# Attention and a routed MLP on one core: scores on 64 rows, whole key tiles per engine, no shifts on GpSimd

## The chip, the cores and the metric

The kernel runs on one core of a Trainium2 chip. The metric is the device time of one execution in microseconds (us). Engines are called TensorE (PE in profile rows, its weight loads PEld), VectorE (DVE), ScalarE (ACT), GpSimd (POOL) and SyncE (SP, which issues the DMAs).

## The reference, cut to what matters

```python
x = A_x                                   # [1, 2048, 448], bf16
xn = layernorm(x)
q = (xn @ wq) -> 16 heads of 28           # k = xn @ wk, v = xn @ wv: ONE key/value head of 28
scores = einsum("bhqd,bkd->bhqk", q, k) * 28 ** -0.5
o = softmax(scores) @ v -> [2048, 448]
h = x + o @ wo
n = layernorm(h); r = n @ w_r             # B: the 8 rows with the largest r go through a gated MLP
out = h + n + scatter(MLP(n[top8]) * sigmoid(r[top8]))
```

All 16 heads share one K and one V. Nearly all of the work is in the scores, their exponentials and the products with V: 16 heads x 2048 queries x 2048 keys.

## The kernel before, in words

**Tiling.** A block b (16 of them, in order) is one group of four heads and 512 queries. Within a block j counts 16 key tiles of 128 keys and i the four heads. So a head tile (b, j, i) is a score tile of 128 keys x 512 queries, which fills one PSUM bank, and there are 1024 of them. Head i of a group sits on partitions 32i to 32i+31 of `Q`; 28 of these 32 rows are the head, one is a constant row that carries an offset. `K` holds K four times, once for each 32 rows. `qk()` is the score matmul of a head tile: 32 rows of K (stationary, 128 columns) against 32 rows of Q (moving, 512 columns).

**Two ways to the exponential.** Tiles of the list `act_tiles` (744) go in pairs through `act_unit`: two `qk()` into two neighbouring banks (0 and 1, or 2 and 3), and one ScalarE exponential over both (line 582) into one of NPB = 8 buffers `P`. Tiles of `dve_tiles` (280) go through `dve_tile`, one at a time, into bank 4 or 5 in turn; VectorE clamps the scores into 16-bit integers that are read as bf16 (line 596, tile `Y`). Four of these make a batch (`dve_batch`), from which three shifted copies are made, each one instruction over 2048 columns (`shift`, line 601): `v == 1`, and `v == 2` in every second batch, on GpSimd, the others on VectorE. The four heads and three key tiles of a batch are spread by a fixed pattern, so every key tile of most blocks has tiles of both kinds.

**Products with V.** Each is a matmul with 128 rows and 32 stationary columns (V with a column of ones, 28 columns of V, zeros); four of them, one for each head i, lie side by side on the columns of the array and are one operation. `act_pv` does this for four tiles of `P`, `dve_pv` for the four tiles of a batch and one of its four copies. They accumulate in bank 6 or 7 (`acc_bank`). That makes 744 + 4 x 280 = 1864 matmuls in 466 groups of four.

**Around the blocks.** `chunk(c)` prepares a quarter of the rows (layer norm, transposes, K, V); its part 0 runs ahead of the first block, the others during it. `q_project` makes Q two blocks ahead. `post_block` moves the sums out of PSUM, inverts the row sums through small DMAs to DRAM and back, and multiplies on GpSimd (line 498). `out_proj` runs for four row tiles after every fourth block, mostly on VectorE. After the last block come the last `out_proj`, the choice of the eight rows, their MLP and the output.

**Order of the work.** `_Graph.op` records every operation with an engine, an assumed duration, its reads and writes, and a priority (its due time, in units of one key tile). `plan()` lays them out as a list schedule and fixes each engine's order; `emit` writes that order out with semaphore waits. So each engine runs a fixed sequence, and an instruction that waits holds up all behind it on its engine. A second, exact program is built behind a flag and runs only when row sums leave a range.

Of the kernel before, what the change touches and what calls it, by code (L numbers as in the profile page):

```python
# [18 lines left out]
class _Op:  # L19
    __slots__ = ("eng", "fns", "dur", "lat", "deps", "prio", "idx", "dma", "start", "end", "sig", "name", "nsucc",  # L20
                 "pred_left", "succs", "ready")


class _Graph:
# [16 lines left out]
    def op(self, eng, fns, dur, reads=(), writes=(), prio=None, dma=False, acc=False, name=""):  # L41
# [34 lines left out]
        return o  # L76

    def plan(self):
# [15 lines left out]
        seq = []  # L94
        while left:
# [18 lines left out]
            c.end = s + c.dur  # L114
            free[e] = c.end
# [109 lines left out]
def _main(nc, G, sb, ps, psb, flag, scr, A_x, A_wq, A_wk, A_wv, A_wo, B_w_r, B_w_gate, B_w_up, B_w_down, out,  # L225
          exact=False):
    S, D, H, C = A_x.shape[1], A_x.shape[2], 16, 8
    DH = D // H
# [4 lines left out]
    NPB = 8  # L233
# [30 lines left out]
    kb = sb("kb", [128, 1], F32)  # L264
    wo_pad = sb("wo_pad", [128, 4, D], BF16)
    Q = sb("Q", [128, 4, 512], BF16)
    K = sb("K", [128, S], BF16)
# [88 lines left out]
    for i in range(4, NT, 4):  # L356
# [64 lines left out]
    def chunk(c):  # L421
# [22 lines left out]
        for t0 in (4 * c, 4 * c + 2):  # L444
# [9 lines left out]
            else:  # L454
# [116 lines left out]
    def qk(bank, tile):  # L571
        b, j, i = tile
        return mm(ps[:, bank, :], K[32 * i:32 * i + 32, j * 128:(j + 1) * 128], Q[32 * i:32 * i + 32, b % 4, :],
                  True, True)

    def act_unit(n, unit):
        b0, sl = 2 * (n % 2), n % NPB
        t = unit[0][0] * 16 + unit[0][1] + unit[0][2] / 8
        G.op(PE, [qk(b0 + k, u) for k, u in enumerate(unit)], 260,
             reads=sorted({("Q", b % 4) for b, j, i in unit}) + sorted({("K", j // 4) for b, j, i in unit}),  # L580
             writes=[pk(b0), pk(b0 + 1)], prio=t - 3)
# [3 lines left out]
    def act_pv(lst):  # L585
        b = lst[0][1][0]
        G.op(PE, [mm(ps[32 * i:32 * i + 32, acc_bank(b), :], Vs[:, 0, j, :], P[:, (n // 2) % NPB, n % 2, :], f, l)
                  for n, (_, j, i), f, l in lst], 260,
             reads=sorted({("P", n // 2 % NPB) for n, *_ in lst}) + sorted({("V", t[1] // 4, 0) for _, t, *_ in lst}),
             writes=[pk(acc_bank(b))])  # L590

    def dve_tile(m, b, j, i):
        n, k, bank = m // 4 % NY, m % 4, 4 + m % 2
        t = b * 16 + j
        G.op(PE, qk(bank, (b, j, i)), 90, reads=[("Q", b % 4), ("K", j // 4)], writes=[pk(bank)], prio=t - 2.9)
        G.op(DV, lambda e: e.tensor_scalar(Y[:, n, 0, k, :].bitcast(I16), ps[:, bank, :], 0.0, 32639.0 - 3 * STEP,  # L596
                                           ALU.max, ALU.min), 610, reads=[pk(bank)], writes=[("Y", n, 0, k)],
             prio=t - 2)
# [12 lines left out]
    def dve_pv(v, lst):
        m, (b, _, _) = lst[0][:2]
        n = m // 4 % NY
        G.op(PE, [mm(ps[32 * i:32 * i + 32, acc_bank(b), :], Vs[:, v + 1, j, :], Y[:, n, v, m % 4, :], f, l)
                  for m, (_, j, i), f, l in lst], 260,
             reads=[("Y", n, v, k) for k in range(4)] + sorted({("V", t[1] // 4, v + 1) for _, t, *_ in lst}),
             writes=[pk(acc_bank(b))])

    for n in range(0, len(act_tiles), 2):
        at(16 * act_tiles[n][0] + act_tiles[n][1] + 0.1, act_unit, n // 2, act_tiles[n:n + 2])  # L620
    quads = []
    for n, tile in enumerate(act_tiles):
        for q in quads[-3:]:
            if len(q) < 4 and q[0][1][0] == tile[0] and all(t[2] != tile[2] for _, t in q):
                q.append((n, tile))
                break
        else:
            quads.append([(n, tile)])
    for q in quads:
        b, j, i = q[-1][1]  # L630
        pv_list.append((16 * b + j + 1.2, 0, 0, q))
    for m in range(0, len(dve_tiles), 4):
        for k in range(4):
            b, j, i = dve_tiles[m + k]
            at(16 * b + j + 0.15, dve_tile, m + k, b, j, i)
        at(16 * b + j + 0.2, dve_batch, m)
        for v in (0, 3, 2, 1):
            pv_list.append((16 * b + j + (3.2 if v == 0 else 3.7 if v == 3 else 4.2 if v == 2 else 4.7), 1, v,
                            [(m + k, dve_tiles[m + k]) for k in range(4)]))
    pv_list.sort(key=lambda t: t[0])  # L640
    first, last = {}, {}
    for n, (tp, kind, v, lst) in enumerate(pv_list):
        for q, e_ in enumerate(lst):
            b, j, i = e_[-1]
            first.setdefault((b, i), (n, q))
            last[b, i] = (n, q)
    for n, (tp, kind, v, lst) in enumerate(pv_list):
        full = [e_ + (first[e_[-1][0], e_[-1][2]] == (n, q), last[e_[-1][0], e_[-1][2]] == (n, q))
                for q, e_ in enumerate(lst)]
        if kind:  # L650
            at(tp, dve_pv, v, full)
        else:
            at(tp, act_pv, full)
# [11 lines left out]
    if exact:  # L665
# [214 lines left out]
```

## Time and profile before

| | |
|---|---|
| median of 3 runs (lowest to highest) | 589.13 us (580.43 to 589.92) |
| the profiled execution | 585.16 us, span 583.3 us |
| TensorE, share of the span busy | 84% |
| VectorE | 72% |
| ScalarE | 65% |
| GpSimd | 43% |
| mean granted clock of TensorE | 0.694 of full speed |

The span runs from the first to the last instruction; the profiled execution takes 1.86 us more than its span. The granted clock of TensorE is 1.00 for 2.4 GHz and 0.50 for 1.2 GHz; other values are means over a stretch with both. A matmul's busy time includes the time to run through the array, so busy TensorE is not TensorE at its peak.

### The profile page before, as it was taken

Reading aid. Unit: us, or ns where it says so; the run is one execution under the profiler, and the core shown is the slowest. Engines: PE = TensorE matmul, PEld = TensorE weight load, DVE = VectorE, ACT = ScalarE, POOL = GpSimd, SP = SyncE. Lnnn points to the kernel's source line nnn. Section 1 sums busy time; section 2 is a strip of 40 time slices with the busy share of each in tenths; the row PEclk is TensorE's granted clock in tenths of the full one; section 3 lists DMA queues with packets and bytes.
Section 4 is the critical chain, followed back from the end, with each engine's and each line's share of the span. In section 5 each row is a group of like instructions: output and inputs, shape, how many; then the busy total and the mean of one; then the engine's idle time right before and its main releaser. Section 6 shows DMA issues by size and latency. Waiting matters only on the chain.

```text
span 583.3 us, 8246 instructions
## 1 busy us (share of the span) xinstructions
PE 487.5 (84%) x3384; PEld 120.7 (21%) x3384; DVE 419.5 (72%) x765; ACT 377.3 (65%) x403; POOL 251.0 (43%) x167
## 2 busy tenths in 40 slices
PE   1889988888797999999896898989998889943286
PEld 1332111221121111112221221211222211111151
DVE  6896256897779875758988888778888876625613
ACT  1586897987667865659776896756569765533102
POOL 6124043767414564426644575563524664320000
PEclk9885577987668665558876995765559865566555
DMA  8900000000000000000000000000000000000003
GB/s 235 269 22 0 21 0 17 5 21 2 19 1 12 9 3 20 0 13 9 21 1 20 1 21 1 20 1 16 6 3 18 2 20 1 20 5 17 1 1 130
DMA packets 15940, 14.64 MB, mean 25 GB/s; under 512 B 5960, under 2 KB 12888, under 8 KB 15896
## 3 DMA queue, kind: packets, MB, share of 16 engines
q1 hardware_dynamic: 15896, 14.05, 8.3%
q8 instruction: 28, 0.46, 0.3%
q14 instruction: 16, 0.13, 0.1%
HBM read 11.94 MB, written 2.10 MB: 24 GB/s over the span
## 4 chain that ended last, share of the span: by engine, by line
PE 60%; DVE 28%; ACT 7%; issue 2%; DMA 1%; POOL 1%; SPq 0%; POOLq 0%; DVEq 0%
PE ps L333 59%; DVE Y L596 9%; DVE Y L601 9%; ACT P L582 6%; DVE junk L547 1%; DMA x_sb<-in_A_x_dram 1%; DVE bn L516 1%; DVE Ot L486 1%; DVE hbuf L514 1%; DVE bn L426 1%; DVE xn L441 1%; DVE Lmn L491 1%; DVE st L530 1%; DVE Q L418 0%; DVE idx L729 0%
## 5 line engine op out<-in xcount | busy, mean ns | idle before, releaser
L582 ACT ACTIVATE P<-ps 128x1024 bf16<-128x1024 f32 x372 | 362.3, 1028 | 140.1 <-PE ps L333 137.6
L601 POOL TENSOR_SCALAR Y<-Y 128x2048 int16<-128x2048 int16 x102 | 206.0, 2032 | 154.7 <-DVE Y L596 154.1
L333 PE MATMUL ps<-Q,K 32*128 32x512 bf16 x1024 | 233.5, 492 | 39.0 <-DVE Y L596 23.5
L596 DVE TENSOR_SCALAR Y<-ps 128x512 int16<-128x512 f32 x280 | 183.3, 681 | 90.0 <-PE ps L333 88.6
L333 PE MATMUL ps<-Y,Vs 128*32 128x512 bf16 x1120 | 133.4, 515 | 3.3 <-DVE Y L601 3.3
L601 DVE TENSOR_SCALAR Y<-Y 128x2048 int16<-128x2048 int16 x108 | 118.8, 1120 | 0.6
L333 PE MATMUL ps<-P,Vs 128*32 128x512 bf16 x744 | 96.2, 512 | 3.0 <-DVE st L518 3.0
L333 PEld LDWEIGHTS ps<-Q,K 32*128 32x128 bf16 x1024 | 46.0, 96 | 230.1 <-ACT P L582 97.7
L498 POOL TENSOR_TENSOR On<-Ot,Rb 128x512 bf16<-128x512 f32 x16 | 22.3, 1392 | 57.8 <-DMA Rb<-l_scr 57.8
L333 PEld LDWEIGHTS ps<-Y,Vs 128*32 128x32 bf16 x1120 | 29.9, 106 | 70.1 <-issue 54.3
L333 PEld LDWEIGHTS ps<-P,Vs 128*32 128x32 bf16 x744 | 20.1, 100 | 66.0 <-issue 61.4
L333 PE MATMUL ps<-wo_pad,On 128*128 128x448 bf16 x64 | 22.6, 501 | 7.2 <-POOL On L498 7.2
L333 PE MATMUL ps<-xnT,wq_pad 112*128 112x512 bf16 x64 | 26.0, 511 | 0.8 <-DVE Ot L486 0.7
L526 POOL TENSOR_TENSOR st<-st,nhalf 128x1 f32<-128x1 f32 x12 | 6.5, 543 | 39.3 <-DVE st L518 39.3
L514 DVE TENSOR_TENSOR hbuf<-ps,x_sb 128x448 f32<-128x448 f32 x16 | 9.8, 611 | 14.3 <-PE ps L333 14.3
L336 PE MATMUL ps<-ident,xn 128*112 128x128 bf16 x64 | 6.7, 271 | 11.8 <-POOL vone L383 10.7
L418 DVE TENSOR_SCALAR Q<-ps,qone 128x512 bf16<-128x512 f32 x16 | 11.7, 731 | 6.0 <-PE ps L333 6.0
L486 DVE COPY Ot<-ps 128x512 f32<-128x512 f32 x15 | 10.3, 684 | 6.3 <-PE ps L333 6.2
L547 DVE SCALAR_TENSOR_TENSOR junk<-hbuf,st,w_rb 128x448 bf16<-128x448 f32 x16 | 14.3, 892 | 0.0
L491 DVE TENSOR_TENSOR Lmn<-Lmn,Lc 128x16 f32<-128x16 f32 x16 | 8.2, 510 | 7.7 <-DMA Lc<-l_scr 7.7
L792 ACT ACTIVATE xnT<-ps 128x448 bf16<-128x448 f32 x8 | 4.3, 543 | 13.1 <-PE ps L333 13.1
L426 DVE BATCH_NORM_STATS2 bn<-x_sb 128x6 f32<-128x448 bf16 x16 | 9.3, 603 | 4.6 <-DMA x_sb<-in_A_x_dram 4.6
(120 smaller groups left out, 185.9 us busy)
## 6 DMA issues: line engine op xcount, KB each, us to landing
Rb<-l_scr SPq DMA_DIRECT2D x16, 256.0 KB
out_dram<-xnT SPq DMA_DIRECT2D x4, 448.0 KB, 3.4
wg_sb<-in_B_w_gate_dram SPq DMA_DIRECT2D x1, 1568.0 KB, 11.9
wu_sb<-in_B_w_up_dram SPq DMA_DIRECT2D x1, 1568.0 KB, 17.6
wd_sb<-in_B_w_down_dram SPq DMA_DIRECT2D x1, 1568.0 KB, 21.5
x_sb<-in_A_x_dram SPq DMA_DIRECT2D x3, 448.0 KB, 6.5
x_sb<-in_A_x_dram SPq DMA_DIRECT2D x2, 224.0 KB, 2.8
wq_sb<-in_A_wq_dram SPq DMA_DIRECT2D x1, 392.0 KB, 5.3
```

What stands on the lines that cost most here:

```text
L333: return lambda e: e.matmul(o, lhsT=l, rhs=r, start=start, stop=stop)
L336: return lambda e: e.transpose(o, i, ident[0:p, 0:p])
L418: G.op(DV, lambda e: e.tensor_scalar(Q[:, b % 4, :], ps[:, bank, :], qone[:, 0:1], None, ALU.add), dvt(512), reads=[pk(bank), "qone"], wri ...
L426: G.op(DV, [lambda e, t=t: e.bn_stats(bn6[:, t, :], x_sb[:, t, :])], dvt(D), reads=[("x", t)], writes=[("bn6", t)])
L486: (lambda e: e.tensor_copy(Ot[:, rb, :], ps[:, acc_bank(b), :])), dvt(512), reads=[pk(acc_bank(b))],
L491: G.op(DV, lambda e: e.tensor_tensor(Lmn[:, :], Lmn[:, :], Lc[:, rb, :], ALU.min), 85, reads=["Lmn", ("Lc", rb)], writes=["Lmn"])
L498: G.op(PO, lambda e: e.tensor_tensor(On[:, qb % 2, g, :], Ot[:, rb, :], Rb[:, rb, :], ALU.mult), 1270, reads=[("Ot", rb), ("Rb", rb)], wri ...
L514: G.op(DV, lambda e: e.tensor_tensor(hbuf[:, hr, :], ps[:, bank, 0:D], x_sb[:, t, :], ALU.add), dvt(D), reads=[pk(bank), ("x", t)], writes ...
L547: G.op(DV, lambda e: e.scalar_tensor_tensor(junk[:, :], hbuf[:, hr, :], st[:, t, 4:5], w_rb[:, :], ALU.mult, ALU.mult, accum_out=st[:, t, ...
L582: G.op(AC, lambda e: e.activation(P[:, sl, :, :], ps[:, b0:b0 + 2, :], ACT.Exp, bias=EBIAS, scale=OCT), 905, reads=[pk(b0), pk(b0 + 1)], w ...
L596: G.op(DV, lambda e: e.tensor_scalar(Y[:, n, 0, k, :].bitcast(I16), ps[:, bank, :], 0.0, 32639.0 - 3 * STEP, ALU.max, ALU.min), 610, reads ...
L601: G.op(eng, lambda e: e.tensor_scalar(Y[:, n, v, :, :].bitcast(I16), Y[:, n, 0, :, :].bitcast(I16), 1.0, v * STEP, ALU.mult, ALU.add), 210 ...
```

## The change

Four things change.

1. **Scores on 64 rows.** `K` becomes two tensors of 128 partitions, `K[:, 0, :]` and `K[:, 1, :]`. In copy p, of each 64 partitions only the 32 that belong to a head of parity p hold K, the other 32 hold zeros. A score matmul takes 64 rows of K and 64 rows of Q (two heads); the zeros take out the head that isn't meant. Two matmuls, on partitions 0 to 63 and 64 to 127, make the scores of heads p and p + 2 and are one operation.
2. **Whole key tiles per engine.** Of each block some key tiles belong to VectorE with all four heads, the others to ScalarE. `groups` gives four such tiles to most blocks, three to blocks 4, 8 and 12, none to block 0: 57 key tiles, 228 head tiles, on VectorE; 199 key tiles, 796 head tiles, on ScalarE. A ScalarE key tile is two `act_unit`s (p = 0, 1), a VectorE key tile two `dve_unit`s, each a pair of scores into banks 4 and 5 and two clamps.
3. **Products with V** are made for the four heads of one key tile at once.
4. **No shifts on GpSimd.** All three shifts of a VectorE key tile run on VectorE, as an addition of a constant.

Beside that NPB falls from 8 to 6; the copies of K take eight operations (one on ScalarE) where there were four; a few one-column operations prepare their scales; and the planner adds 100 ns where TensorE goes from one form (scores, products, other) to another.

```diff
-    NPB = 8
+    NPB = 6
...
+            if e == PE:
+                if form != c.form:
+                    c.end += 100.0
+                form = c.form
...
+    G.op(DV, lambda e: e.tensor_single_scalar(pid2[:, :], pidx[:, :], 63, ALU.bitwise_and), 70, reads=["pidx"],
+         writes=["pid2"])
...
+    for p in range(2):
+        G.op(DV, lambda e, p=p: e.tensor_scalar(ksc[:, p:p + 1], pid2[:, :], 32, KSCALE,
+                                                ALU.is_ge if p else ALU.is_lt, ALU.mult), 70, reads=["pid2"],
+             writes=[("ksc", p)])
+        G.op(DV, lambda e, p=p: e.tensor_scalar(kb[:, p:p + 1], pid2[:, :], DH + 32 * p, ZERO, ALU.is_equal, ALU.mult),
+             70, reads=["pid2"], writes=[("kb", p)])
...
-        G.op(DV, lambda e, bank=bank, c=c: e.tensor_scalar(K[:, c * 512:(c + 1) * 512], ps[:, bank, :], KSCALE, kb[:, 0:1],
-                                                           ALU.mult, ALU.add), dvt(512),
-             reads=[pk(bank), "kb0"], writes=[("K", c)])
+        for p in range(2):
+            if c == 0 and p == 0:
+                G.op(AC, lambda e, bank=bank, p=p: e.activation(K[:, p, 0:512], ps[:, bank, :], ACT.Identity,
+                                                                bias=kb[:, p:p + 1], scale=ksc[:, p:p + 1]), 640,
+                     reads=[pk(bank), ("kb", p), ("ksc", p)], writes=[("K", c, p)])
+            else:
+                G.op(DV, lambda e, bank=bank, c=c, p=p: e.tensor_scalar(
+                    K[:, p, c * 512:(c + 1) * 512], ps[:, bank, :], ksc[:, p:p + 1], kb[:, p:p + 1],
+                    ALU.mult, ALU.add), 670, reads=[pk(bank), ("kb", p), ("ksc", p)], writes=[("K", c, p)])
...
-    triples = [(0, 1, 2, 3, 4)] * NB
-    triples[0] = ()
-    triples[1] = (0, 2, 4)
+    groups = [4] * NB
+    groups[0] = 0
     for b in range(4, NB, 4):
-        triples[b] = (0, 1, 2, 4)
+        groups[b] = 3
+    where = {0: (), 1: (9,), 2: (5, 11), 3: (3, 7, 11), 4: (1, 5, 9, 13)}
...
+    def qk(bank, b, j, p):
+        return [mm(ps[:, bank + k, :], K[64 * k:64 * k + 64, p, j * 128:(j + 1) * 128],
+                   Q[64 * k:64 * k + 64, b % 4, :], True, True) for k in range(2)]
...
+    def act_pv(n, b, j, f, l):
+        G.op(PE, [mm(ps[32 * i:32 * i + 32, acc_bank(b), :], Vs[:, 0, j, :], P[:, (2 * n + i % 2) % NPB, i // 2, :], f, l)
+                  for i in range(4)], 216,
+             reads=[("P", 2 * n % NPB), ("P", (2 * n + 1) % NPB), ("V", j // 4, 0)], writes=[pk(acc_bank(b))], form=2)
+
+    def dve_unit(m, b, j, p, t):
+        n = m % NY
+        G.op(PE, qk(4, b, j, p), 216, reads=[("Q", b % 4), ("K", j // 4, p)], writes=[pk(4), pk(5)], prio=t - 2.9,
+             form=1)
+        for k in range(2):
+            G.op(DV, lambda e, k=k: e.tensor_scalar(Y[:, n, 0, p + 2 * k, :].bitcast(I16), ps[:, 4 + k, :], 0.0,
+                                                    32639.0 - 3 * STEP, ALU.max, ALU.min), 610, reads=[pk(4 + k)],
+                 writes=[("Y", n, 0, p + 2 * k)], prio=t - 2)
+
+    def shift(m, v):
+        n = m % NY
+        G.op(DV, lambda e: e.tensor_scalar(Y[:, n, v, :, :].bitcast(I16), Y[:, n, 0, :, :].bitcast(I16),
+                                           v * STEP, None, ALU.add), 610,
              reads=[("Y", n, 0, k) for k in range(4)], writes=[("Y", n, v, k) for k in range(4)])
...
+    for n, (b, j, t) in enumerate(act_tiles):
+        for p in range(2):
+            at(t + 0.6 * p, act_unit, 2 * n + p, b, j, p, t + 0.6 * p)
+        pv_list.append((t + 2.0, act_pv, n, b, j))
+    for m, (b, j, t) in enumerate(dve_tiles):
+        for p in range(2):
+            at(t + 1.5 * p, dve_unit, m, b, j, p, t + 1.5 * p)
         for v in (1, 2, 3):
+            at(t + 1.6 + 0.5 * v, shift, m, v)
+        for v in range(4):
+            pv_list.append((t + 2.2 + 0.5 * v, dve_pv, m, v, b, j))
```

## Rows read from the trace of the kernel before

**Rows 1.** The page: span, busy time of each engine, chain that ended last.
```profile
span 583.3 us, 8246 instructions
...
PE 487.5 (84%) x3384; PEld 120.7 (21%) x3384; DVE 419.5 (72%) x765; ACT 377.3 (65%) x403; POOL 251.0 (43%) x167
...
PE 60%; DVE 28%; ACT 7%; issue 2%; DMA 1%; POOL 1%; SPq 0%; POOLq 0%; DVEq 0%
```
**Rows 2.** Windows: stretch, length, busy time (instructions), granted clock, DMA share, GB/s.
```profile
321.50:352.20 30.70, 27.20 (x251) 7.09 (x248) 27.69 (x42) 26.88 (x28) 20.07 (x10) 1.00 0.03 10
208.90:266.90 58.00, 56.93 (x314) 9.81 (x313) 36.48 (x57) 33.62 (x35) 26.15 (x15) 0.50 0.03 11
99.70:120.10 20.40, 16.34 (x168) 4.37 (x166) 17.48 (x24) 19.18 (x20) 14.08 (x7) 1.00 0.04 14
300.00:320.00 20.00, 14.85 (x103) 3.73 (x99) 18.48 (x51) 14.13 (x16) 7.87 (x8) 0.78 0.05 16
```
**Rows 3.** Groups by line, 208.9 to 266.9 us: count, busy us, mean ns, idle before.
```profile
L333 PE MATMUL ps<-Q,K 32*128 32x512 bf16 x102 | 30.1, 604 | 1.1 <-DVE Y L596 0.6 <-ACT P L582 0.3
```
**Rows 4.** The same group, 321.5 to 352.2 us.
```profile
L333 PE MATMUL ps<-Q,K 32*128 32x512 bf16 x83 | 16.6, 390 | 2.2 <-DVE Y L596 1.2 <-ACT P L582 0.8
```
**Rows 5.** Timeline: the first and the last exponential on ScalarE.
```profile
19.02 1.02 ACT L582 ACTIVATE P<-ps 128x1024 bf16<-128x1024 f32 x1 [6.23 <-PE ps L333]
...
514.16 1.02 ACT L582 ACTIVATE P<-ps 128x1024 bf16<-128x1024 f32 x1 [0.42 <-PE ps L333]
```
**Rows 6.** Windows of TensorE, only instructions that read Q: the scores.
```profile
79.00:82.60 3.60, 1.26 (x6) 0.50 0.00 0
82.60:86.00 3.40, 2.14 (x12) 1.00 0.00 0
478.50:482.00 3.50, 1.82 (x11) 0.99 0.00 0
235.00:239.60 4.60, 3.27 (x12) 0.50 0.00 0
```
**Rows 7.** Windows of TensorE, only instructions that read Vs: the products with V.
```profile
79.00:82.60 3.60, 2.54 (x24) 0.50 0.00 0
82.60:86.00 3.40, 1.06 (x12) 1.00 0.00 0
```
**Rows 8.** TensorE near the end of the span: a timeline row, and a window.
```profile
562.63 5.09 PE L333 MATMUL ps<-wd_sb,guT 128*8 128x448 bf16 x14 [1.02 <-DVE guT L775]
...
567.30:568.40 1.10, 0.41 (x2) 1.00 0.00 0
```
**Rows 9.** Timeline of TensorE at 2.4 GHz: start, length, what.
```profile
341.10 0.39 PE L333 MATMUL ps<-P,Vs 128*32 128x512 bf16 x4
...
341.31 0.39 PE L333 MATMUL ps<-Y,Vs 128*32 128x512 bf16 x4
...
341.63 0.39 PE L333 MATMUL ps<-Q,K 32*128 32x512 bf16 x2
```
**Rows 10.** Timeline of TensorE at 1.2 GHz.
```profile
68.36 0.61 PE L333 MATMUL ps<-Q,K 32*128 32x512 bf16 x2 [0.31 <-ACT P L582]
68.90 0.62 PE L333 MATMUL ps<-P,Vs 128*32 128x512 bf16 x4
```
**Rows 11.** The page: exponentials, shifts and clamps over the whole span.
```profile
L582 ACT ACTIVATE P<-ps 128x1024 bf16<-128x1024 f32 x372 | 362.3, 1028 | 140.1 <-PE ps L333 137.6
L601 POOL TENSOR_SCALAR Y<-Y 128x2048 int16<-128x2048 int16 x102 | 206.0, 2032 | 154.7 <-DVE Y L596 154.1
...
L596 DVE TENSOR_SCALAR Y<-ps 128x512 int16<-128x512 f32 x280 | 183.3, 681 | 90.0 <-PE ps L333 88.6
...
L601 DVE TENSOR_SCALAR Y<-Y 128x2048 int16<-128x2048 int16 x108 | 118.8, 1120 | 0.6
```
**Rows 12.** Timeline of VectorE: the last three shifts, with GpSimd at rest.
```profile
511.44 1.90 DVE L601 TENSOR_SCALAR Y<-Y 128x2048 int16<-128x2048 int16 x3
```
**Rows 13.** Timeline of VectorE: the first copy of K.
```profile
15.64 0.75 DVE L461 TENSOR_SCALAR K<-ps,kb 128x512 bf16<-128x512 f32 x1 [0.79 <-PE ps L333]
```

More of the change, by code (lines that the diff above doesn't have):

```diff
@@ L20 @@
     __slots__ = ("eng", "fns", "dur", "lat", "deps", "prio", "idx", "dma", "start", "end", "sig", "name", "nsucc",
-                 "pred_left", "succs", "ready")
+                 "pred_left", "succs", "ready", "form")
 class _Graph:
@@ L39, in __init__, with op @@
         self.orders = None
-    def op(self, eng, fns, dur, reads=(), writes=(), prio=None, dma=False, acc=False, name=""):
+    def op(self, eng, fns, dur, reads=(), writes=(), prio=None, dma=False, acc=False, name="", form=0):
         o = _Op()
@@ L49, in op @@
         o.sig = False
+        o.form = form
         def need(p, sem):
@@ L94, in plan @@
         seq = []
+        form = 0
         while left:
@@ L263, in _main @@
     qone = sb("qone", [128, 1], F32)
-    kb = sb("kb", [128, 1], F32)
+    kb = sb("kb", [128, 2], F32)
+    ksc = sb("ksc", [128, 2], F32)
+    pid2 = sb("pid2", [128, 1], I32)
     wo_pad = sb("wo_pad", [128, 4, D], BF16)
     Q = sb("Q", [128, 4, 512], BF16)
-    K = sb("K", [128, S], BF16)
+    K = sb("K", [128, 2, S], BF16)
     Vs = sb("Vs", [128, NV, NT, 32], BF16)
@@ L552, in out_proj @@
              reads=[("st6", t), "sw", ("st2", t)], writes=[("r", t)])
-    triples = [(0, 1, 2, 3, 4)] * NB
-    triples[0] = ()
-    triples[1] = (0, 2, 4)
+    groups = [4] * NB
+    groups[0] = 0
     for b in range(4, NB, 4):
-        triples[b] = (0, 1, 2, 4)
+        groups[b] = 3
+    where = {0: (), 1: (9,), 2: (5, 11), 3: (3, 7, 11), 4: (1, 5, 9, 13)}
     dve_tiles, act_tiles = [], []
     for b in range(NB):
+        d = where[groups[b]]
         for j in range(NT):
-            for i in range(4):
-                on_dve = j < 15 and j // 3 in triples[b] and (j % 3, i) in ((0, 2), (1, 1), (2, 0), (2, 3))
-                (dve_tiles if on_dve else act_tiles).append((b, j, i))
+            if j in d:
+                dve_tiles.append((b, j, 16.0 * b + j - 0.5))
+            else:
+                act_tiles.append((b, j, 16.0 * (b + (j - sum(k < j for k in d)) / (NT - len(d)))))
     events = [(4.0 * c - 9.0, lambda c=c: chunk(c)) for c in range(4)]
@@ L569, in at, with act_unit @@
         events.append((t, lambda: fn(*a)))
[L571 to L576, printed above, removed]
+    def qk(bank, b, j, p):
+        return [mm(ps[:, bank + k, :], K[64 * k:64 * k + 64, p, j * 128:(j + 1) * 128],
+                   Q[64 * k:64 * k + 64, b % 4, :], True, True) for k in range(2)]
+    def act_unit(n, b, j, p, t):
@@ L577, in act_unit @@
         b0, sl = 2 * (n % 2), n % NPB
[L578 to L581, printed above, removed]
+        G.op(PE, qk(b0, b, j, p), 216, reads=[("Q", b % 4), ("K", j // 4, p)], writes=[pk(b0), pk(b0 + 1)],
+             prio=t - 3, form=1)
         G.op(AC, lambda e: e.activation(P[:, sl, :, :], ps[:, b0:b0 + 2, :], ACT.Exp, bias=EBIAS, scale=OCT),
@@ L583, in act_unit @@
              905, reads=[pk(b0), pk(b0 + 1)], writes=[("P", sl)], prio=t)
[L585 to L598, printed above, removed]
@@ L600, in shift @@
-    def shift(n, v, eng):
-        G.op(eng, lambda e: e.tensor_scalar(Y[:, n, v, :, :].bitcast(I16), Y[:, n, 0, :, :].bitcast(I16), 1.0,
-                                            v * STEP, ALU.mult, ALU.add), 2100 if eng == PO else 610,
-             reads=[("Y", n, 0, k) for k in range(4)], writes=[("Y", n, v, k) for k in range(4)])
-    def dve_batch(m):
-        n, q = m // 4 % NY, m // 4
-        last = q >= len(dve_tiles) // 4 - 2
-        for v in (1, 2, 3):
-            shift(n, v, PO if (v == 1 or (v == 2 and q % 2)) and not last else DV)
@@ L611, in dve_pv @@
[L611 to L639, printed above, removed]
@@ L640, in _main @@
-    pv_list.sort(key=lambda t: t[0])
[L641 to L653, printed above, removed]
+    def act_pv(n, b, j, f, l):
+        G.op(PE, [mm(ps[32 * i:32 * i + 32, acc_bank(b), :], Vs[:, 0, j, :], P[:, (2 * n + i % 2) % NPB, i // 2, :], f, l)
+                  for i in range(4)], 216,
+             reads=[("P", 2 * n % NPB), ("P", (2 * n + 1) % NPB), ("V", j // 4, 0)], writes=[pk(acc_bank(b))], form=2)
@@ new lines, in shift, with dve_pv @@
+    def shift(m, v):
+        n = m % NY
+        G.op(DV, lambda e: e.tensor_scalar(Y[:, n, v, :, :].bitcast(I16), Y[:, n, 0, :, :].bitcast(I16),
+                                           v * STEP, None, ALU.add), 610,
+             reads=[("Y", n, 0, k) for k in range(4)], writes=[("Y", n, v, k) for k in range(4)])
+    def dve_pv(m, v, b, j, f, l):
+        n = m % NY
+        G.op(PE, [mm(ps[32 * i:32 * i + 32, acc_bank(b), :], Vs[:, v + 1, j, :], Y[:, n, v, i, :], f, l)
+                  for i in range(4)], 216,
+             reads=[("Y", n, v, k) for k in range(4)] + [("V", j // 4, v + 1)], writes=[pk(acc_bank(b))], form=2)
@@ L654, in _main @@
+    pv_list.sort(key=lambda t: t[0])
     done = {}
-    for tp, kind, v, lst in pv_list:
-        done[lst[0][1][0]] = tp
+    for n, e_ in enumerate(pv_list):
+        b = e_[-2]
+        at(e_[0], e_[1], *e_[2:], b not in done, n == max(k for k, q in enumerate(pv_list) if q[-2] == b))
+        done[b] = e_[0]
     for b in range(NB):
@@ L676, in _main @@
                     nx += 1
-                    G.op(PE, [mm(ps[:, c, :], Q[rows, b % 4, k * 128:(k + 1) * 128], K[rows, c * 512:(c + 1) * 512],
+                    G.op(PE, [mm(ps[:, c, :], Q[rows, b % 4, k * 128:(k + 1) * 128], K[rows, i % 2, c * 512:(c + 1) * 512],
                                  True, True) for c in range(4)], 1000,
-                         reads=[("Q", b % 4)] + [("K", c) for c in range(4)], writes=[pk(c) for c in range(4)])
+                         reads=[("Q", b % 4)] + [("K", c, i % 2) for c in range(4)], writes=[pk(c) for c in range(4)])
                     G.op(DV, lambda e, r2=r2: e.tensor_reduce(nmax[:, r2:r2 + 1], ps[:, 0:4, :], AX.XY, ALU.max,
```

2 lines of the change are left out of this document (removed).

## The prediction

> **What bounds the kernel now.** I read the page first: busy shares and the chain that ended last. TensorE is busy 487.5 of 583.3 us and carries 60% of the chain, VectorE 28%, ScalarE 7% [rows 1]. An average over stretches with different limits says little, so the windows came next, cut where the granted clock of TensorE changes [rows 2]. From 208.9 to 266.9 us the clock is 1.2 GHz and TensorE is busy 56.9 of 58.0 us, ScalarE 33.6: TensorE alone is the bound. From 321.5 to 352.2 us it is 2.4 GHz, and VectorE (27.7 of 30.7 us), TensorE (27.2) and ScalarE (26.9) are all nearly full, so none is.
>
> What the clock is worth follows from the score matmuls in these stretches, one for each head tile: 102 in 58.0 us is 0.569 us a tile at 1.2 GHz [rows 2, 3], 83 in 30.7 us is 0.370 us at 2.4 GHz [rows 2, 4]. The loop over the blocks runs from the first exponential at 19.0 to the end of the last at 515.2 us [rows 5], 496 us for 1024 tiles. All at 1.2 GHz it would take 582 us, all at 2.4 GHz 379; 496 lies at a share of 0.58 of the tiles at 1.2 GHz. So the loop is set by its clock more than by any one engine, and the change has to be judged at each level, and then by what it does to the share.
>
> **The clock.** What did TensorE do before it rose or fell? From 79.0 to 82.6 us the clock was low and TensorE spent 2.5 us in products with V (128 rows) and 1.3 us in scores (32 rows); at 82.6 it rose [rows 6, 7]. In the next 3.4 us it did 2.1 us of scores and 1.1 us of products [rows 6, 7], and the clock fell. The stretch 478.5 to 482.0 us, nearly all scores, ended in a fall as well [rows 6]. From 235.0 to 239.6 us there were 3.3 us of scores, two thirds of the time, and the clock stayed low [rows 6]; so it did through the whole of 208.9 to 266.9 us, at 98% busy [rows 2]. Near the end of the span 14 matmuls of 448 columns took 5.09 us, 0.36 us each, which is the low level; they use 128 rows but only 8 stationary columns, and behind them the clock stood at 2.4 GHz [rows 8]. So in this trace rises come behind stretches with many rows at work, falls behind stretches of 32-row scores. After the change a pair of scores works on all 128 rows (64 and 64), half of them against zeros. I read this as: the scores will look like the products do now. The trace can't show whether zeros in the stationary operand take that away; the 8-column row is the nearest, and speaks for rows rather than filled cells.
>
> The Trainium skill (TensorE: Matmul & The Clock Gate, Why this matters for your kernels) says that for the full clock TensorE is to be kept busy without a break. The 58 us at 98% busy and 1.2 GHz don't agree with that alone. By that rule the change, which takes work from TensorE, would do nothing for the clock; that is the first rival below.
>
> **The change part by part.**
>
> *Scores and products on TensorE.* A turn from one form to another costs time: at 2.4 GHz one group of four products follows another after 0.21 us, but scores follow products after 0.32 us [rows 9], so a turn is 0.11 us. At 1.2 GHz products follow scores after 0.54 us [rows 10], 0.43 us without the turn. For 64-row scores no row exists. Bounds: side by side as the 32-row pair now (one slot a pair, [rows 9]) or one after the other (two slots). I take one slot, since the two halves share no rows and the row is of the same kind. Slots after: 512 pairs of scores, 199 + 57 x 4 = 427 groups of products (466 before), 64 Q projections and 48 output projections inside the loop: 1051. Turns: two for each group of products at most, 854; some groups stand together, so I take 700, 77 us (0 to 94). At 2.4 GHz that is 1051 x 0.21 + 77 = 298 us, beside ScalarE and off the path. At 1.2 GHz it is 1051 x 0.43 + 77 = 529, with 2% of waits [rows 2] 540 us, against 582 before.
>
> The Trainium skill (TensorE: Matmul & The Clock Gate, Measured speedup vs the span model) gives 3.07 times for four 32-row tiles side by side, which 64 rows rule out: scores at that rate would be an estimated 70 us where 512 x 0.21 gives 108. In the trace pairs are what the kernel issues, so that is not lost now; at 2.4 GHz it would be off the path anyway.
>
> *ScalarE.* 796 head tiles are 398 exponentials where there were 372. At 2.4 GHz 28 of them took 26.88 us, 0.96 each [rows 2]; 398 make 382 us. This is the largest load of any engine, so at 2.4 GHz ScalarE sets the loop. How full can it be? 0.88 in one stretch at 2.4 GHz and 0.94 in another [rows 2]. I take 0.93, near the better, because VectorE, which was just as full there, is relieved; 0.88 and 0.97 are the ends. 382 / 0.93 = 411 us (394 to 434). Note that this is more than the 379 us of now: at the high clock the change loses.
>
> *VectorE and GpSimd.* Clamps: 280 in 183.3 us, 0.655 each [rows 11]; 228 make 149. Shifts: 108 on VectorE at a mean of 1.12 us, while GpSimd did 102 others at 2.03 [rows 11]; the last three on VectorE, with GpSimd at rest, took 1.90 us, 0.63 each [rows 12]. So 171 shifts make 108 us, fewer than the 119 of now, if GpSimd's absence is what makes them short; at the mean of now they would be 191. I take 0.63, since GpSimd is left only the small work of line 498 and a few one-column operations. The rest, 419.5 - 183.3 - 118.8 = 117 us, stays. Three more copies of K at 0.75 [rows 13] and four one-column operations add 3. Sum 377 us over the whole span, under ScalarE.
>
> *The pair of banks 4 and 5.* Before, they went round one by one; now a pair of scores waits for both clamps of the pair before it, and on TensorE all that is queued behind it waits too, exponentials' scores among it. An uncovered wait is about 0.39 us of matmul [rows 9] and a hand-over, say 0.5 us, 114 times: 57 us. The cover is the three shifts of the key tile before (1.9 us), which have due times between the two pairs. I put it at nothing; uncovered it makes VectorE 434 us.
>
> *The rest.* NPB from 8 to 6: the products of a key tile must be done before the third tile after it; at 0.96 us an exponential that leaves some 3.8 us, and TensorE has slack at 2.4 GHz. Nothing, or part of the 0.88 above. The first copy of K is split over two engines and the copies of later chunks lie in block 0, which has no VectorE tiles; one copy, 0.8 us, goes on the path to the first exponential (0 to 0.8). The one-column operations run while x is being loaded.
>
> **The sum.** I don't expect the clock to be high throughout: when TensorE waits for ScalarE it rests more. I take a tenth of the tiles at 1.2 GHz: 411 + 0.1 x (540 - 411) = 424 us. Ahead of the loop 19.0 + 0.8, behind it 583.3 - 515.2 = 68.1, outside the span 1.9: 514 us, against 585.2 of the profiled execution, which itself is 0.7% under the median of 589.1.
>
> **The rivals.**
>
> *The clock goes its old way* (chance 0.12). The share of tiles at 1.2 GHz stays 0.58: 411 + 0.58 x 129 = 486, in all 576 us, 2% under the median. For it: nothing in the trace shows that rows with zeros count. Against it: the rises and falls above [rows 6 to 8]. It is what the rule quoted above from the Trainium skill (TensorE: Matmul & The Clock Gate) would give.
>
> *TensorE rests so much beside ScalarE that the clock never rises* (0.06). The loop then takes TensorE's 540 us, in all 630, slower. It passes 601 us (2% over the median) where the share at 1.2 GHz is above 0.78. For it: at 2.4 GHz TensorE has only 298 of 411 us of work. Against it: at 1.2 GHz its work fills the time, 128 rows wide, and the trace shows rises behind such stretches.
>
> *VectorE, or scores that don't run side by side* (0.14). With the wait on banks 4 and 5 uncovered VectorE has 434 us; from 300 to 320 us, with an output projection, it is already busy 18.5 of 20 against 14.1 of ScalarE [rows 2]. Or 512 more slots of 0.21 us bring TensorE to 407 us. Either makes the loop some 440 us, in all 530.
>
> **How the numbers follow.** The forecast has 0.68. Its ends are ScalarE at 0.97 full with a high clock throughout, 394 + 90 = 484 us, and 434 with a fifth low, 545. The range runs from 485 to 577, past the first rival, and leaves out the second and a little on the fast side. About 2% is what a measurement of this kernel can tell from no change. Faster by more than that: 0.68 + 0.14 + a third of the first rival, 0.86; within 2%: 0.08; slower: 0.06.
>
> **What the profile after would show.** Granted clock near 0.9 or more through the loop, where it was 0.69 over the span; ScalarE busy over 0.9 of each stretch in the loop; waits of ScalarE for TensorE well under the 138 us of now [rows 11]; shifts at 0.6 to 0.65 us; scores in pairs, each pair one slot. The prediction is wrong if stretches at 1.2 GHz with TensorE full remain, or if the clamps wait for their scores after every pair.

## The result, and the profile after

| | before | after |
|---|---|---|
| median of 4 runs (lowest to highest) | 588.92 us (580.43 to 589.92) | 473.06 us (470.2 to 475.65) |
| profiled execution, its span | 585.16, 583.3 us | 475.65, 473.9 us |
| mean granted clock | 0.694 | 0.924 |

The ratio is 0.807, interval 0.797 to 0.817. The chip runs some executions in a slower state, at a lower clock, so the table of experiments has, beside the median of all runs, the mean of the runs outside that state, and differences between runs are taken from these means. The direction was forecast; the time lies 41 us under the predicted 514 and 12 under the range.

The page of the changed kernel, the same lines as [rows 1], and the granted clock in 40 slices:

```profile
span 473.9 us, 7880 instructions
...
PE 365.2 (77%) x3228; PEld 111.1 (23%) x3228; DVE 372.3 (79%) x783; ACT 385.8 (81%) x430; POOL 47.1 (10%) x65
...
PEclk9988799999999999999999999998999999766565
...
ACT 41%; DVE 24%; PE 22%; DMA 7%; issue 3%; POOL 2%; SPq 0%; POOLq 0%; DVEq 0%
```

ScalarE has taken TensorE's place at the head of the chain (41%), and the clock is high in nearly every slice up to the end of the loop. The windows (columns as in [rows 2]) show a loop with one bound over most of its length:

```profile
60.00:400.00 340.00, 289.89 (x2634) 78.96 (x2638) 301.10 (x583) 331.22 (x359) 29.30 (x27) 0.99 0.05 14
160.00:180.00 20.00, 17.06 (x169) 4.74 (x168) 18.02 (x34) 20.00 (x23) 1.28 (x1) 1.00 0.05 16
320.00:340.00 20.00, 16.42 (x128) 4.45 (x128) 14.44 (x38) 16.39 (x19) 3.11 (x4) 0.91 0.04 14
```

ScalarE is busy 331 of 340 us, and without a break from 160 to 180 us; from 320 to 340 us it isn't (see g1). Its runs on the timeline, against [rows 5]:

```profile
19.99 5.61 ACT L601 ACTIVATE P<-ps 128x1024 bf16<-128x1024 f32 x6 [3.61 <-PE ps L341]
...
79.31 21.30 ACT L601 ACTIVATE P<-ps 128x1024 bf16<-128x1024 f32 x23
...
392.83 14.04 ACT L601 ACTIVATE P<-ps 128x1024 bf16<-128x1024 f32 x15
```

The loop runs from 20.0 to 406.9 us, 387 us where it was 496 and where I had put 424. Ahead of it lie 20.0 us (predicted 19.8), behind it 67.0 (68.1): the whole miss is in the loop. The groups, against [rows 4, 11]:

```profile
L601 ACT ACTIVATE P<-ps 128x1024 bf16<-128x1024 f32 x398 | 370.0, 1094 | 20.5 <-PE ps L341 19.1
L341 PE MATMUL ps<-Q,K 64*128 64x512 bf16 x1024 | 186.6, 391 | 48.4 <-ACT P L601 31.2 <-DVE Y L614 9.4 <-DVE K L481 2.1
L614 DVE TENSOR_SCALAR Y<-ps 128x512 int16<-128x512 f32 x228 | 146.9, 681 | 21.5 <-PE ps L341 21.1
L620 DVE TENSOR_SCALAR Y<-Y 128x2048 int16<-128x2048 int16 x171 | 118.4, 731 | 1.6
```

ScalarE waits 19 us for TensorE in all, where it was 138. Before its scores TensorE waits mostly for ScalarE (31 of 48 us).

### The profile page after: what moved, and what is told of

It is laid out like the page before. It is cut to its first block, busy times and chain, and to the rows that moved or that the text cites. A ratio compares the mean times of both kernels' runs of the same rounds, so it can differ in the third digit from the quotient of the medians.

```text
span 473.9 us, 7880 instructions
## 1 busy us (share of the span) xinstructions
PE 365.2 (77%) x3228; PEld 111.1 (23%) x3228; DVE 372.3 (79%) x783; ACT 385.8 (81%) x430; POOL 47.1 (10%) x65
## 4 chain that ended last, share of the span: by engine, by line
ACT 41%; DVE 24%; PE 22%; DMA 7%; issue 3%; POOL 2%; SPq 0%; POOLq 0%; DVEq 0%
ACT P L601 40%; PE ps L341 22%; DVE Y L614 8%; DVE Y L620 6%; DMA Rb<-l_scr 3%; DMA x_sb<-in_A_x_dram 1%; DVE Ot L506 1%; POOL On L518 1%; DVE K L481 1%; DVE bn L440 1%; DMA l_scr<-Lc 1%; DVE xnT L469 1%; DVE Vs L492 1%; PE ps L344 1%; DVE xn L455 1%
## 5 line engine op out<-in xcount | busy, mean ns | idle before, releaser
L601 ACT ACTIVATE P<-ps 128x1024 bf16<-128x1024 f32 x398 | 370.0, 1094 | 20.5 <-PE ps L341 19.1
L341 PE MATMUL ps<-Q,K 64*128 64x512 bf16 x1024 | 186.6, 391 | 48.4 <-ACT P L601 31.2
L614 DVE TENSOR_SCALAR Y<-ps 128x512 int16<-128x512 f32 x228 | 146.9, 681 | 21.5 <-PE ps L341 21.1
L620 DVE TENSOR_SCALAR Y<-Y 128x2048 int16<-128x2048 int16 x171 | 118.4, 731 | 1.6
L341 PEld LDWEIGHTS ps<-Q,K 64*128 64x128 bf16 x1024 | 45.0, 93 | 196.5 <-ACT P L601 147.9
L341 PE MATMUL ps<-P,Vs 128*32 128x512 bf16 x796 | 80.6, 395 | 0.7 <-ACT P L601 0.7
L341 PE MATMUL ps<-Y,Vs 128*32 128x512 bf16 x912 | 72.2, 381 | 0.0
L341 PE MATMUL ps<-wo_pad,On 128*128 128x448 bf16 x64 | 17.9, 399 | 12.7 <-POOL On L518 12.7
L341 PEld LDWEIGHTS ps<-Y,Vs 128*32 128x32 bf16 x912 | 23.1, 96 | 17.0 <-issue 7.2
L341 PE MATMUL ps<-xnT,wq_pad 112*128 112x512 bf16 x64 | 21.4, 430 | 2.9 <-DVE Ot L506 2.7
L511 DVE TENSOR_TENSOR Lmn<-Lmn,Lc 128x16 f32<-128x16 f32 x16 | 2.7, 169 | 14.5 <-DMA Lc<-l_scr 14.5
```

The source lines that it names most:

```text
L341: return lambda e: e.matmul(o, lhsT=l, rhs=r, start=start, stop=stop)
L614: G.op(DV, lambda e, k=k: e.tensor_scalar(Y[:, n, 0, p + 2 * k, :].bitcast(I16), ps[:, 4 + k, :], 0.0, 32639.0 - 3 * STEP, ALU.max, ALU.mi ...
L620: G.op(DV, lambda e: e.tensor_scalar(Y[:, n, v, :, :].bitcast(I16), Y[:, n, 0, :, :].bitcast(I16), v * STEP, None, ALU.add), 610, reads=[( ...
```

## The experiments

Old structure means mixed key tiles in batches as before; new structure means whole key tiles, with the paired scores for VectorE, the planner's 100 ns and the first copy of K on two engines that came with them. "Loop" is from the first exponential to the end of the last in the profiled execution, whose time is given and can be above the mean; "clock" is the granted clock from 60 to 400 us there. Ratios are against the kernel before on the same chip; its mean is 586 to 588 us in every session but the last (i1 and g2: a single run, 578.5), so means of runs that did not run together can be compared too. Only e1 against the changed kernel, and e2 against e3, keep every engine's order of instructions. The other edits let the planner lay out a new order, so what is put down to them is the edit together with its order.

| run | structure, rows | head tiles on VectorE | GpSimd shifts | median us | mean us | ratio (interval) | profiled us | loop us | clock |
|---|---|---|---|---|---|---|---|---|---|
| before | old, 32 | 280 | 102 | 588.9 | 586.1 | 1 | 585.2 | 496 | 0.72 |
| e3 | old, 32 | 280 | 102 | 588.9 | 585.7 | 0.992 (0.986 to 0.998) | 580.8 | 493 | 0.71 |
| e2 | old, 64 | 280 | 102 | 536.0 | 530.6 | 0.893 (0.885 to 0.900) | 538.4 | 451 | 0.92 |
| f1 | old, 64 | 280 | 0 | 533.5 | 532.8 | 0.899 (0.891 to 0.907) | 541.4 | 448 | 0.94 |
| h1 | old, 64 | 228 | 0 | 483.4 | 481.7 | 0.819 (0.806 to 0.832) | 486.0 | 398 | 0.97 |
| after | new, 64 | 228 | 0 | 473.1 | 473.0 | 0.807 (0.797 to 0.817) | 475.7 | 387 | 0.99 |
| h2 | new, 64 | 280 | 0 | 506.7 | 506.7 | 0.861 (0.854 to 0.868) | 507.3 | 416 | 0.95 |
| e4 | new, 64 | 228 | 55 | 491.2 | 491.4 | 0.828 (0.824 to 0.832) | 489.4 | 401 | 0.98 |
| e1 | new, 32 | 228 | 0 | 502.2 | 502.0 | 0.845 (0.840 to 0.849) | 513.4 | 426 | 0.82 |

**e1: 32 rows in the changed kernel.** Each engine's order of instructions stays the same.

```diff
-        return [mm(ps[:, bank + k, :], K[64 * k:64 * k + 64, p, j * 128:(j + 1) * 128],
-                   Q[64 * k:64 * k + 64, b % 4, :], True, True) for k in range(2)]
+        return [mm(ps[:, bank + k, :], K[64 * k + 32 * p:64 * k + 32 * p + 32, p, j * 128:(j + 1) * 128],
+                   Q[64 * k + 32 * p:64 * k + 32 * p + 32, b % 4, :], True, True) for k in range(2)]
```

> The changed kernel with one edit: each score matmul takes only the 32 rows of its head, not 64 with zeros; order, pairs, waits and all other work stay. Theory (the 64 rows hold the clock at 2.4 GHz): stretches at 1.2 GHz come back, a mean clock of 0.65 to 0.85 instead of 0.92, and with TensorE's 540 us as the loop of a clock that is always low against 387 measured, a time of 505 to 560 us. Rival (the clock is high because TensorE was relieved and every operation is a pair or four): the clock stays over 0.9 and the time at 473 us, within 2%.

502.2 us, 29 more, just under the theory's range. The window:

```profile
60.00:400.00 340.00, 303.26 (x2386) 73.22 (x2382) 271.75 (x529) 306.29 (x326) 26.30 (x25) 0.82 0.04 12
```

With the rows as the only difference, TensorE is busier (303 us of 340 against 290) and its clock lower (0.82 against 0.99). This execution, 513.4 us, is the longest of e1; in those of 500.5 to 504.5 us the clock over the whole span is 0.79 to 0.82, against 0.92 to 0.94 for the changed kernel. The rival falls as stated, but so does half of the theory: the 32-row kernel still has a much better clock and time than before.

**e2 and e3: 64 rows in the kernel before, and its control.** e2 takes over the two copies of K and their scales, orders the heads of a ScalarE pair so that they lie on different halves, and has 6 buffers of P. e3 is e2 with 32 rows per matmul and the same order on every engine.

```diff
-            for i in range(4):
+            for i in ((0, 3, 1, 2), (2, 0, 3, 1), (1, 2, 0, 3))[j % 3]:
...
-        return mm(ps[:, bank, :], K[32 * i:32 * i + 32, j * 128:(j + 1) * 128], Q[32 * i:32 * i + 32, b % 4, :],
-                  True, True)
+        return mm(ps[:, bank, :], K[64 * (i // 2):64 * (i // 2) + 64, i % 2, j * 128:(j + 1) * 128],
+                  Q[64 * (i // 2):64 * (i // 2) + 64, b % 4, :], True, True)
```

> The kernel before with only the scores changed: 64 rows with zero-padded copies of K, the tiles of a ScalarE pair reordered so that they lie on different halves, 6 buffers of P for room. Mixed key tiles, GpSimd shifts and single scores for VectorE stay. Theory (rows set the clock, the clock sets the loop): the clock goes over 0.85, and the loop near its 379 us at 2.4 GHz: 465 to 500 us. Rival (the gain needs whole key tiles and no GpSimd shifts): within 3% of 589 us.

> The kernel of e2 with each score matmul on its own 32 rows again, same order, buffers and copies of K: the control. Theory: clock near 0.69 and 575 to 605 us, as before. Rival: like e2, since only the rows differ.

The control lies at the kernel before; e2 is 55 us under it. First the window of e2, then, in a fence of its own, that of e3:

```profile
60.00:400.00 340.00, 294.76 (x2356) 74.32 (x2352) 297.25 (x492) 275.54 (x288) 192.28 (x105) 0.92 0.04 12
```

```profile
60.00:400.00 340.00, 308.57 (x2164) 66.92 (x2166) 263.67 (x429) 252.01 (x262) 175.18 (x96) 0.71 0.03 10
```

The rows alone lift the clock from 0.71 to 0.92 (over the whole span of the runs behind the means, from 0.67 to 0.69 up to 0.87 to 0.88). But the time misses the theory's range: the loop takes 451 us, not the 379 that I had read from stretches at 2.4 GHz: in e2 ScalarE waits 97 us for TensorE, and VectorE leads its chain:

```profile
L591 ACT ACTIVATE P<-ps 128x1024 bf16<-128x1024 f32 x372 | 357.5, 1037 | 99.6 <-PE ps L335 97.0
...
DVE 42%; PE 37%; ACT 9%; DMA 5%; issue 3%; POOL 3%; SPq 0%; POOLq 0%; DVEq 0%
```

**e4: one shift of three back on GpSimd.**

```diff
-        G.op(DV, lambda e: e.tensor_scalar(Y[:, n, v, :, :].bitcast(I16), Y[:, n, 0, :, :].bitcast(I16),
-                                           v * STEP, None, ALU.add), 610,
+        eng = PO if v == 1 and m < len(dve_tiles) - 2 else DV
+        G.op(eng, lambda e: e.tensor_scalar(Y[:, n, v, :, :].bitcast(I16), Y[:, n, 0, :, :].bitcast(I16), 1.0,
+                                            v * STEP, ALU.mult, ALU.add), 1950 if eng == PO else 610,
```

> The changed kernel with the first of the three shifts of each VectorE key tile (all but the last two) on GpSimd again, 55 in all. Theory (ScalarE bounds the loop, shifts are off the path): VectorE's other shifts grow from 0.69 to 0.9 us or more where both run, the time stays within 2% of 473 us. Rival (taking the shifts from GpSimd was a large part of the gain): slower by 4% or more, 492 us and over.

491.2 us, 18 more (3.9%): between the two, nearer to the rival. The groups of e4:

```profile
L621 DVE TENSOR_SCALAR Y<-Y 128x2048 int16<-128x2048 int16 x116 | 133.6, 1172 | 1.5
L621 POOL TENSOR_SCALAR Y<-Y 128x2048 int16<-128x2048 int16 x55 | 126.2, 2296 | 155.3 <-DVE Y L614 143.2 <-DVE mv L537 8.4 <-DVE st L538 3.7
```

116 shifts on VectorE take 134 us, where all 171 took 118. GpSimd's help costs VectorE more than it takes off. The edit also writes the shift with a multiplication by 1, the form of the kernel before; that isn't what makes it long, since f1 (below) runs 210 of that form without GpSimd at 0.66 us each. The timeline shows where the time goes: two shifts beside one of GpSimd, and two with GpSimd at rest.

```profile
34.72 3.00 DVE L621 TENSOR_SCALAR Y<-Y 128x2048 int16<-128x2048 int16 x2
34.77 2.40 POOL L621 TENSOR_SCALAR Y<-Y 128x2048 int16<-128x2048 int16 x1 [3.23 <-DVE Y L614]
...
172.22 1.28 DVE L621 TENSOR_SCALAR Y<-Y 128x2048 int16<-128x2048 int16 x2
```

Over the whole trace 48 of the 116 take over 1 us, 1.83 in the mean, and each of these overlaps a GpSimd shift; the other 68 take 0.71. Not every overlap is long: 41 of the 68 overlap one too.

**f1 and f2: no GpSimd shifts in the old structure**, with 64 rows (f1) and with 32 (f2).

```diff
-            shift(n, v, PO if (v == 1 or (v == 2 and q % 2)) and not last else DV)
+            shift(n, v, DV)
```

> The kernel of e2 (the old structure with 64-row scores, 536 us) with all three shifts of every batch on VectorE, 210 in all; mixed key tiles and VectorE's share of 280 head tiles stay. Theory now (two parts of equal rank: the rows give the clock, taking the shifts from GpSimd relieves VectorE, which was 42% of e2's chain): shifts at 0.65 to 0.75 us instead of 1.24, VectorE's busy time no higher than e2's 431 us, 500 to 518 us. Rival (the whole key tiles, with fewer head tiles on VectorE, are what is left): 525 us and over.

> The kernel before (32 rows, mixed key tiles) with all shifts on VectorE and nothing else changed. If at the low clock TensorE alone sets the pace, shifts cost nothing there and the time stays within 2% of 589 us, with a clock near 0.69. If GpSimd's shifts hold the loop up at either clock, 570 us or less.

```profile
L610 DVE TENSOR_SCALAR Y<-Y 128x2048 int16<-128x2048 int16 x210 | 138.5, 711 | 0.3
```

f1 took 533.5 us: the shifts shrank to 0.66 us each (138.5 for 210) and VectorE's total was 424, as expected, but the time stayed (mean 532.8 against e2's 530.6), so the theory's step failed. f2 took 634 us (624 to 644), slower than before by some 7%, which neither case had. In its profile (644 us, its longest run) the clock from 60 to 400 us is 0.59 and ScalarE waits 191 us for TensorE. The edit makes the planner lay out other orders; which of these differences lowers the clock I haven't separated.

**h1: VectorE's share in the old structure**, from 70 batches to 57.

```diff
-    triples = [(0, 1, 2, 3, 4)] * NB
+    triples = [(0, 1, 3, 4)] * NB
     triples[0] = ()
-    triples[1] = (0, 2, 4)
     for b in range(4, NB, 4):
-        triples[b] = (0, 1, 2, 4)
+        triples[b] = (0, 2, 4)
```

> The kernel of f1 (old structure, 64 rows, no GpSimd shifts, 533 us) with 57 batches for VectorE instead of 70, so 228 head tiles as in the changed kernel; mixed key tiles stay. Theory (whole key tiles matter by themselves: in the mixed order each engine waits for the other through TensorE's order): 510 us or more. Rival (VectorE's share was what was left): 470 to 490 us.

483.4 us: the rival's range. 13 batches fewer are worth 51 us. The window of f1, then that of h1:

```profile
60.00:400.00 340.00, 288.11 (x2339) 73.25 (x2335) 289.40 (x571) 271.19 (x284) 24.95 (x24) 0.94 0.04 11
```

```profile
60.00:400.00 340.00, 301.02 (x2556) 80.92 (x2560) 293.46 (x570) 324.06 (x350) 24.87 (x26) 0.97 0.04 13
```

In f1 no engine is full (85% at most) and ScalarE is at 0.80; in h1 ScalarE is at 0.95. So the share counts, but by what wait it holds f1 up these rows don't show.

**h2: VectorE's old share in the new structure**, 70 whole key tiles.

```diff
-    groups = [4] * NB
+    groups = [5] * NB
+    groups[1] = groups[2] = 4
     groups[0] = 0
     for b in range(4, NB, 4):
-        groups[b] = 3
+        groups[b] = 4
-    where = {0: (), 1: (9,), 2: (5, 11), 3: (3, 7, 11), 4: (1, 5, 9, 13)}
+    where = {0: (), 1: (9,), 2: (5, 11), 3: (3, 7, 11), 4: (1, 5, 9, 13), 5: (1, 4, 7, 10, 13)}
```

> The changed kernel with 70 whole key tiles for VectorE instead of 57, 280 head tiles as before. VectorE then has some 430 us of work and ScalarE 372 exponentials. Theory (whole key tiles are what counts, VectorE's share adds its load): VectorE becomes the bound, 485 to 500 us. Rival (the share was what was left between f1 and the changed kernel): 515 us and over, close to f1.

506.7 us, 34 more, between the two cases, nearer to the theory's. VectorE is now the bound, as the window and the chain of h2 say (busy 315 of 340 us):

```profile
60.00:400.00 340.00, 292.48 (x2533) 76.80 (x2536) 314.72 (x612) 286.29 (x305) 27.91 (x25) 0.95 0.04 12
...
DVE 63%; PE 14%; ACT 11%; DMA 5%; POOL 2%; issue 2%; SPq 0%; POOLq 0%; DVEq 0%
```

Against f1 with the same share, the new structure takes the mean from 532.8 to 506.7 us; with the small share (h1 to after) from 481.7 to 473.0, where the intervals of the ratios overlap.

**i1: the small share alone in the kernel before** (h1's edit; 32 rows, GpSimd shifts).

> The kernel before (32 rows, mixed key tiles, GpSimd shifts) with 57 batches for VectorE instead of 70 and nothing else changed. TensorE has 156 products fewer, 39 groups of 0.43 us at 1.2 GHz, and 26 pairs in place of 52 single scores, 11 us: if at the low clock TensorE's load sets the loop, 555 to 575 us with a clock near 0.70. Rival (the share relieves VectorE and so lifts the clock too): under 550 us and a clock over 0.75. Third: no change, within 2% of 589 us.

565 to 576 us against 578 to 611 on its chip, median 570, clock 0.70 from 60 to 400 us: the first case. The size of the gain is uncertain: the mean is 568.4 us, and the kernel before has 578.5 here (one run) and 586 to 588 elsewhere. It is 10 to 18 us where the same step is worth 51 in f1; that it is what TensorE saves at the low clock is argued, not shown.

**f3: VectorE's scores one at a time; h3: the same with 32 rows.**

```diff
-        G.op(PE, qk(4, b, j, p), 216, reads=[("Q", b % 4), ("K", j // 4, p)], writes=[pk(4), pk(5)], prio=t - 2.9,
-             form=1)
         for k in range(2):
+            G.op(PE, qk(4, b, j, p)[k], 216, reads=[("Q", b % 4), ("K", j // 4, p)], writes=[pk(4 + k)], prio=t - 2.9,
+                 form=1)
```

> The changed kernel with the pair of scores for VectorE issued as two operations, each waiting only for its own bank's clamp. If the wait on both banks cost nothing, as I put it: within 2% of 473 us, perhaps a little slower by more slots and turns. If the pair's wait was a cost that another gain hid: 463 us or less.

> The changed kernel with 32-row scores (as e1, 502 us, clock 0.82) and VectorE's scores one at a time (as f3, 470 us). Theory of the clock (it falls behind stretches in which few rows work): single 32-row scores put fewer rows to work than pairs, so a clock under 0.80 and 510 us or more. Rival (the pairing plays no part in the clock): 495 to 504 us with a clock of 0.82.

f3: 469.5 us, 0.7% under the changed kernel, ratio 0.793 (0.785 to 0.801): the wait on both banks costs next to nothing. h3: 509.1 us, ratio 0.862 (0.849 to 0.875), against e1's 0.845 (0.840 to 0.849); the time lies between the two cases. Its clock from 60 to 400 us is 0.82, e1's own, both in the longest run of each; over the whole span of the other runs it is 0.77 to 0.79 against e1's 0.79 to 0.82. Too little to say that the pairs raise the clock.

**g1, g3, g2: what is left.** From 318 us the chain of the changed kernel is not ScalarE:

```profile
320.36 5.26 DMA Rb<-l_scr
...
325.69 1.69 POOL On L518
327.38 0.05 issue
327.43 4.67 PE ps L341 x24
```

and ScalarE's timeline has a hole there:

```profile
329.69 2.10 ACT L601 ACTIVATE P<-ps 128x1024 bf16<-128x1024 f32 x2 [3.21 <-PE ps L341]
```

An output projection waits in TensorE's order for the row sums, whose last DMA takes 5 us where the plan assumes 2; the scores behind it wait too. g1 plans it with 6.5:

```diff
         dma(Rb[:, rb, :], scr[b, 1].unsqueeze(1).broadcast_to([4, 32, 512]), [("Rb", rb)], reads=[("scr1", b)])
+            lat=6500.0)
```

> The changed kernel with one number in the plan: the DMA that brings the inverted row sums back is planned with 6.5 us instead of 2.0. In the changed kernel the output projections stand too early in TensorE's order and ScalarE rests behind them for 1.9, 1.7 and 3.2 us. Theory: these three rests go, 462 to 469 us. Rival (something else is late next): within 1% of 473 us.

465.3 us, ratio 0.785 (0.779 to 0.792), 8 under the changed kernel; the loop is 376 us, the three rests are gone from ScalarE's timeline, and its wait for TensorE falls to half:

```profile
L602 ACT ACTIVATE P<-ps 128x1024 bf16<-128x1024 f32 x398 | 368.1, 1109 | 11.1 <-PE ps L341 10.1
```

g3 adds f3's edit, g2 a fifth key tile for VectorE in blocks 2, 6 and 10.

> The changed kernel with both edits that made it faster: the planned 6.5 us for the DMA of the row sums (465 us alone) and VectorE's scores one at a time (470 us alone). If the two are separate rests of ScalarE, their gains add: 458 to 464 us. If ScalarE's 398 exponentials at 0.92 us leave nothing more: within 0.5% of 465 us.

> The kernel of g1 (465 us) with a fifth key tile for VectorE in blocks 2, 6 and 10, 60 in all. ScalarE has 6 exponentials fewer, 5.5 us; VectorE has 13.5 us more, in blocks without output projections, where it has some 10% idle. If ScalarE alone bounds these blocks: 458 to 463 us. If the two are at the balance point: 463 to 468 us. If VectorE becomes the bound there: 470 us and over.

g3: 467.5 us (465.2 to 470.4), just past the second case: the two gains don't add. g2: 463.6 us (463.3 to 465.1), the best median of all, where its first two ranges meet; g1 ran from 461.2 to 467.3, so the two can't be told apart. Both beat the changed kernel.

## Why the prediction was wrong

**The clock: right.** The first rival (its old way) and the second (always low) both fell. The rise and fall read from [rows 6 to 8] held in e1 against after and e3 against e2, each pair with the same order on every engine. Rows with zeros count. (The zeros stand in K alone and meet Q's rows of another head, so which of the two operands counts isn't shown.) TensorE is busy 89% at a mean clock of 0.82 in e1, 85% at 0.99 after, and in e3 it is busy 30.0 of the 30 us from 320 to 350 us at 0.50. So the advice to keep TensorE busy without a break for the full clock (the Trainium skill, TensorE: Matmul & The Clock Gate, Why this matters for your kernels) isn't enough here by itself.

**The size of the ScalarE term: wrong, and it put the time out of the range.** I priced an exponential at 0.96 us from a stretch, 321.5 to 352.2 us, in which ScalarE kept stopping (28 exponentials in seven runs), and so paid the start of each run again. The timeline of before had it:

```profile
333.45 1.02 ACT L582 ACTIVATE P<-ps 128x1024 bf16<-128x1024 f32 x1 [0.61 <-PE ps L333]
335.18 1.94 ACT L582 ACTIVATE P<-ps 128x1024 bf16<-128x1024 f32 x2 [0.71 <-PE ps L333]
```

One takes 1.02 us, the second of a run adds 0.92. After, 23 unbroken take 21.30 us: (21.30 - 1.09) / 22 = 0.92 a step. Over the loop it is 370.0 / 398 = 0.93. The fill, 0.93 predicted, was 370 / 387 = 0.956. So 382 / 0.93 = 411 became 387, 24 us, 13 by the price and 11 by the fill; the tenth of the tiles at 1.2 GHz, 13 us, didn't come either (17 of the 387 us were low, most of them before 60 us). 24 + 13 is the 37 us by which the loop is shorter. The range failed with it: its low end used 0.96 too, and with 0.93 it would have been 471 us, under the measured 473.

**"All at 2.4 GHz it would take 379 us; at the high clock the change loses": wrong.** I made a rate for the whole loop from one stretch of 30.7 us without an output projection. e2 and f1 run the old structure at a clock of 0.92 to 0.94 and take 451 and 448 us, where my two rates mixed to those clocks would give about 400. The old share of VectorE costs time there: moving 52 head tiles to ScalarE, which I had counted as a loss on ScalarE, is worth 51 us (f1 to h1). In means the main path is: rows 55 us (e3 to e2), the GpSimd shifts nothing at the point where they were taken out (530.6 to 532.8), share 51, whole key tiles and what came with them 9. The order matters: the share alone in the kernel before gives 570 us (i1), and one GpSimd shift put back into the changed kernel costs 18 (e4).

**The smaller steps.** One slot for a pair of 64-row scores held: on TensorE's timeline after, a pair is followed by a projection 0.32 us later, as in [rows 9].

```profile
84.27 0.39 PE L341 MATMUL ps<-Q,K 64*128 64x512 bf16 x2
84.59 0.60 PE L341 MATMUL ps<-xnT,wq_pad 112*128 112x512 bf16 x2
```

VectorE came to 372 us (377 predicted), its shifts to 0.69 each (0.63) and the clamps to 0.64 (0.655). The wait on banks 4 and 5 costs nothing to speak of (f3). The shifts lie above the 0.60 to 0.65 us that the forecast asked to see, and 0.9 of each stretch for ScalarE isn't reached from 320 to 340 us (0.82). One sum has a slip: 298 + 512 x 0.21 is 406 us, not 407; nothing rests on it. Missed altogether: the output projections, which the faster loop brings ahead of the DMA that they wait for (g1).

**Open:** why the new structure has a clock of 0.82 with 32 rows (e1) where the old has 0.71 (e3). The share alone doesn't do it (i1, 0.70), nor can pairing be shown to (h3). And why f2 is slower than the kernel before, and what holds f1 up with no engine full.

## What to carry to other kernels

When a loop goes between two clocks, find what TensorE does ahead of rises and falls, and test it with a pair of kernels that differ in nothing else. Rates from one good stretch are no rates of a loop: take the price of a saturated engine from its longest unbroken run, and look for the engine that fills up elsewhere. When the pace rises, an assumed latency in a static order that was harmless becomes a stop of the engine that now bounds.

## What the runs showed of the hardware

- Rows of a score matmul that carry zeros count for the granted clock: 0.99 against 0.82 (after, e1), 0.92 against 0.71 (e2, e3), from 60 to 400 us, the same order of instructions within each pair.
- A shift on GpSimd slows VectorE's own by more than it saves: 116 beside GpSimd's 55 took 133.6 us (e4), 171 alone 118.4 (after). In e4 every shift over 1 us (48, 1.83 us in the mean) overlaps one of GpSimd.
- Exponentials over 1024 columns step at 0.92 us in unbroken runs (after), while the mean duration of one is 1.09 us, against 1.03 before.
